# A spectral and state-space network on one core: rounding moved into PSUM, constant products taken out, instruction orders replaced

## The chip, the core and the metric

The kernel runs on one core of a Trainium2 chip. The core has a matrix engine, TensorE (PE in the profile, with its weight loads as PEld), which writes only to the accumulator memory PSUM; VectorE (DVE), ScalarE (ACT) and GpSimd (POOL), which work elementwise; and SyncE (SP), which here only issues transfers (DMAs) between the chip's main memory (HBM) and the on-chip memory SBUF. Each engine runs its own instructions in a fixed order and waits for the others through semaphores. The metric is the device time of one execution in microseconds, lower is better; the figure for the kernel before is the median of three timed runs.

## The reference

Four layers with a residual each, on `x` of 2048 rows and 512 columns. Layer A is a two-dimensional real FFT, a product with stored complex weights and the inverse FFT. Layer B is a diagonal state-space model (SSM): from parameters of 512 channels and 128 states it makes a convolution kernel `K` of length 2048 for each channel, and convolves with it by FFTs of length 4096. The normalized input goes into both. `K` is the same in both B layers.

```python
def _A_ref(x, w_r, w_i):
    X = jnp.fft.rfft2(x, axes=(-2, -1))
    return jnp.fft.irfft2(X * (w_r + 1j * w_i), s=(S, D), axes=(-2, -1))

def _B_ref(u, log_A_real, A_imag, C_real, C_imag, log_dt, D_skip):
    A = -jnp.exp(log_A_real) + 1j * A_imag
    C = (C_real + 1j * C_imag) * dt[:, None]
    P = jnp.exp((A * dt[:, None])[:, :, None] * pos[None, None, :])
    K = 2.0 * jnp.einsum("dn,dnl->dl", C, P).real
    Kf, Uf = jnp.fft.rfft(K, 2 * L), jnp.fft.rfft(u_t, 2 * L)
    y = jnp.fft.irfft(Uf * Kf[None, :, :], 2 * L)[:, :, :L]
    return y.transpose(0, 2, 1) + u * D_skip[None, None, :]

x = x + _A_ref(_layernorm(x), A_w_r, A_w_i)
x = x + _B_ref(_layernorm(x), ...)
x = x + _A_ref(_layernorm(x), A_w_r, A_w_i)
x = x + _B_ref(_layernorm(x), ...)
```

## The kernel before

All FFTs are products with small tables of sines and cosines on TensorE. Nearly every product is made in two halves (`halves`, L330, and `side_by_side`, L336): 64 columns of weights go to the left half of TensorE's array and 64 to the right half, and two such products run side by side. Products over 128 rows use two such halves of 128 by 64; some products of layer B and of the SSM's transform (those with the table `t`) use only 64 rows and run four at a time as 64 by 64. The profile names these shapes 128*64 and 64*64. A float32 product shows as two rows in the profile.

Layer A runs in three steps of 16 to 18 rounds: `spread` (layer norm and the first transform), `middle` (`forward`, `weigh`, `back`: the second transform, the product with the weights on DVE, the way back) and `end` (`fold`, `rows_back`). Layer B runs over four blocks of 128 channels: `rows` (64-row products), a copy by ACT and a transpose by DVE to the tile `z`, `pair` (products `p<-z,mb`), `weigh` (DVE products with `K`'s transform, then sums of 64x512 on POOL or DVE to `u`), and back through `units` (`p<-mb,u`) and `rows` (`p<-u,t`).

The SSM kernel is made beside the first layers A and B. `kernel_parts` turns the parameters into bfloat16 parts, written to HBM and read back as `th`. `kernel_time` then goes over 32 units of 16 channels, in groups of four, each unit in two halves, so 64 half units. Of each unit `grow` makes magnitudes: products `pk<-kb,th` of 512 columns, exponentials on ACT to `mag`. Of each half unit `bend` (L853) makes the phase, counted in turns, in one PSUM bank, `pk`: two pairs of products of 256 columns (`pk<-kb,th`). To bring it near zero DVE rounds the phase to the next integer (L864, `kw<-pk`: add and subtract 1.5 times 2 to the 23rd, `MAGIC`), and TensorE subtracts the integer from the same bank by a pair of products with minus the identity (`pk<-kw,ni`, 512 columns). Then ACT takes the absolute value and the sine (`sine`, `kf<-pk` and `pk<-pk`) and the cosine (`qp<-kf`), DVE multiplies with the magnitudes (`terms`, L886 and L888), and TensorE sums over the states (`total`, L899, `pv<-qp`). There are three `pk` banks and one `pv` bank. `kernel_freq` transforms `K` and stores it.

The order of the instructions is written out: `TURNS` holds for each engine a list of numbers, positions of the instructions as the program text makes them, and `take_turns` sets each engine's order by it. `ROOMS` holds, for every tile that the pools give out, which of the buffers of its name it takes. `WARM` holds, for some PSUM tiles, how many pairs of products of a constant (`self.warm`, ones) are made into the tile ahead of its real products (in `ps`); they are overwritten and nobody reads them. There are 231 such pairs, 924 rows in the profile. Transfers are issued by SP in its own order; the constants `kb` and `ni` are sent by POOL's queue, since they are converted to bfloat16 on the way.

Of the kernel before, what the change touches and what calls it, by code (L numbers as in the profile page):

```python
# [12 lines left out]
ALU = mybir.AluOpType  # L13
# [78 lines left out]
def constants():  # L92
# [111 lines left out]
    out["ni"] = -np.eye(128)  # L204
    out["kb"] = kb.reshape(96, 2560)
# [47 lines left out]
class Net:  # L253
# [553 lines left out]
    def kernel_constants(self):  # L807

        BF = mybir.dt.bfloat16
        self.kb = self.sb("kb", [2560], dt=BF, rows=96)  # L810
        self.ni = self.sb("ni", [128], dt=BF)
        self.nc.gpsimd.dma_start(self.kb, self.cst["kb"])
        self.nc.gpsimd.dma_start(self.ni, self.cst["ni"])

    def kernel_time(self, parts, kt, units, group):
# [6 lines left out]
        KQ, RM, RN, KP, RP = (KB[:, k:k + 512] for k in range(0, 2560, 512))  # L822
# [32 lines left out]
        def bend(i, j):  # L855
# [8 lines left out]
            nc.vector.tensor_scalar(whole, p, MAGIC, -MAGIC, op0=ALU.add, op1=ALU.add)  # L864
            self.halves(p, self.ni, whole, start=False, stop=True, skip_group_check=True)
            live[i, j] = p, mag

        def sine(i, j):
# [3 lines left out]
            ordered(p, p, ACT.Sin, scale=-TAU)  # L872
# [251 lines left out]
def net_kernel(ctx, tc, x, w, ends, kin, log_dt, d_skip, out, **cst):  # L1124
# [19 lines left out]
    with ExitStack() as outer:  # L1144
        with ExitStack() as early:
            early.enter_context(net.phase("pk", P, pk=(2048, PK), pv=(2048, PV)))
            with net.phase("p", P, p1=(2048, 8 - PK - PV), p2="p1", p3="p1"), \
                    net.phase("a", x=(32768, 1), ta=(8192, 1), ca=(6912, 1), u=(16384, 2), w=(2056, WA), wt=(2056, WT),
                              wv="w", junk="w"):
                A = net.layer_a(w, src=xv, dst=hd)  # L1150
                early.enter_context(net.phase("k0", side="right", kb=(5120, 1), ni=(256, 1), th=(1536, TH)))
                net.kernel_constants()
                with net.phase("v", val=(10240, 1), hp=(HP, 2)):
# [5 lines left out]
                    early.enter_context(net.phase("k", side="right", kw=(1024, 2), mag=(6144, MAG),  # L1159
# [10 lines left out]
            outer.enter_context(net.phase("b", t2=(8192, 1), u=(16384, 2), kk=(2048, 8), ta="t2", wt="w", wb="w", xw="w"))  # L1170
# [61 lines left out]
0-17 23-24 18-19 25-28 20-21 32-39 22 29-31 40-65 67-70 76-79 66 80-81 71-72 82-83 73-75 85-88 94-95 84 89-92  # L1232
103-106 93 96-97 112-113 107-108 98-101 109-110 102 114-115 111 116-119 121-124 120 125-126 130-131 127-128
132-133 129 134-161 172-179 163-168 180-181 169-171 182-193 162 194-211 218-219 234-235 212-217 220-221 236-241
222-225 242-249 256-259 226-231 260 264-266 250 267 251 261 232 268-272 252 262 273 253 263 233 274-279 298-307
280-281 254 312 282 286 255 313 287 314 288 315 289 283-285 308-311 316-321 290-291 322-331 338-339 292-295
340-342 346-349 343-345 296-297 350-351 332-335 366-371 358-365 336-337 374-387 414-417 372-373 402-413 418-423
464-465 424-427 388-393 448-451 466-467 452-455 476-483 512-513 456-461 514-515 394-397 516-517 398-401 462-463
428-431 518-519 432-433 520-523 434 436-437 435 438-439 352-357 548-551 554-557 524-525 468-475 552-553 440-441
484-487 558 492-494 504 495 559 505-507 488-491 442-447 496-497 526-533 498-499 508-511 500-503 534-543 560-561  # L1240
544-547 562-564 568 580 569 581 570 582 571 583 565-567 606-609 572-573 586-593 574-577 584 594 578 612 579 595
613 585 610 596-597 611 614-617 620-621 618-619 598-599 626-627 600-601 622-623 628 634-635 629-630 636-637
631-633 654-657 602-605 638-639 660-667 624-625 640-643 658 668-670 688 671 689 659 690-691 646-651 672-673
652-653 644-645 674-677 694-701 678 702-704 692 705 693 679 738-741 706-711 680-685 752-757 712 760 758 761 759
713 742-743 686 762-763 687 764-771 798-800 808-809 801-807 810-811 772-773 812 834-837 813-815 714-721 774-775
784-785 816-819 838-839 786-787 722-729 788-791 840-843 792-795 730-737 844-845 796-797 820-823 826-831 854-857
878 900-902 832-833 744-749 858-863 750-751 910 824-825 846-849 776-777 850-851 778-783 942 903 852-853 904-906
879-880 886-887 864-875 888 881-884 907-908 943-944 894-896 889-890 945 876-877 946-948 885 909 897 911-912
891-893 926-936 949 898 937-938 913-914 939 915-917 899 970-973 940-941 918-925 974-975 962-969 950-961 976-983
986-987 1032-1033 988-989 984-985 990-997 1006-1009 1034-1035 1010-1015 1054-1055 998-1003 1036-1039 1004-1005  # L1250
1056-1057 1076-1077 1040-1043 1016-1023 1044-1045 1066-1067 1024-1031 1078-1081 1068-1075 1046-1051 1082-1083
# [296 lines left out]
```

## Time and profile before

| | us |
|---|---|
| median of three timed runs | 716.46 |
| the three runs | 716.46, 710.45, 718.14 |
| span of the profiled execution, first to last instruction | 713.4 |

The profiled execution has no time of its own beside its span; the span lies inside the spread of the three runs, 3.1 us below their median.

The profile names an engine's instructions by line, operation, the tiles written and read and their shapes, with a count; "busy us, mean ns" are the time in which at least one of the group ran and the mean duration of one. Since products overlap, a group's busy time is less than count times mean. After it stand the engine's idle time just before these instructions and who ended it. In the tables of windows each engine's busy time stands with its number of instructions, then the share of TensorE's full clock that was granted (PEclk), the mean busy share of the DMA engines and the GB/s moved. A timeline row has a start, a duration, the engine, the line and the number of instructions merged into it.

### The profile page before, as it was taken

What the parts mean: (1) busy time and instruction counts of PE and PEld (TensorE: products, weight loads), DVE (VectorE), ACT (ScalarE), POOL (GpSimd) and SP (SyncE); (2) the same over time, 40 slices, a digit from 0 to 9 for tenths busy, and PEclk for the clock granted to TensorE, in tenths of its full rate; (3) what the DMA queues carried; (4) which work ended last, traced back from release to release, by engine and by line L of the source; (5) the groups of instructions that cost most, each with busy time, mean ns of one, the idle gap of its engine ahead of it and who ended that gap; (6) DMA issues with size and microseconds to landing.
All of it is one profiled execution on the core that took longest, in us unless ns stands there. A gap on an engine that the chain in (4) does not pass through costs nothing. (4 is left out here: it accounts for less than half of the span.)

```text
span 713.4 us, 23503 instructions
## 1 busy us (share of the span) xinstructions
PE 626.0 (88%) x9580; PEld 491.3 (69%) x9580; DVE 601.9 (84%) x1348; ACT 438.2 (61%) x946; POOL 357.3 (50%) x565
## 2 busy tenths in 40 slices
PE   4459989989996999889999997984989899999996
PEld 3237867878674867667858876774877766577876
DVE  4998497998999799969999676869588699799993
ACT  3558999997664796778868524333767427333322
POOL 1533528672852704543196356452056484286870
PEclk9779999999999999999999999997999999999999
DMA  8602611613558350455544689222123103335514
GB/s 282 229 0 89 210 48 47 122 62 43 167 133 245 107 138 32 65 128 94 163 62 136 195 198 246 80 106 75 61 77 89 46 2 104 125 103 149 156 34 111
DMA packets 137355, 81.32 MB, mean 114 GB/s; under 512 B 70976, under 2 KB 116928, under 8 KB 136352
## 3 DMA queue, kind: packets, MB, share of 16 engines
q1 hardware_dynamic: 136992, 79.30, 40.1%
q8 instruction: 76, 1.25, 0.7%
q0 software_dynamic: 256, 0.52, 0.4%
q14 instruction: 31, 0.25, 0.1%
HBM read 54.90 MB, written 25.43 MB: 113 GB/s over the span
## 5 line engine op out<-in xcount | busy, mean ns | idle before, releaser
L1003 POOL TENSOR_TENSOR u<-wb,wb 64x512 f32<-64x512 f32 x90 | 123.2, 1373 | 66.0 <-DVE wb L991 60.9
L336 PE MATMUL p<-z,mb 128*64 128x512 f32 (+2 forms) x480 | 108.0, 517 | 1.7 <-DVE wb L991 1.3
L899 PE MATMUL pv<-qp 128*64 128x128 f32 x1024 | 81.6, 279 | 5.0 <-ACT stage L907 4.2
L991 DVE TENSOR_TENSOR wb<-p,kk 128x512 f32<-128x512 f32 x128 | 81.5, 676 | 4.3 <-POOL u L1003 2.3
L336 PEld LDWEIGHTS p<-mb,u 128*64 128x64 f32 x2048 | 73.1, 138 | 13.1 <-issue 6.7
L336 PE MATMUL p<-mb,u 128*64 128x64 f32 x2048 | 74.3, 223 | 4.4 <-issue 2.0
L663 ACT COPY z<-p 128x512 f32<-128x512 f32 x96 | 52.4, 595 | 41.8 <-PE p L336 31.6
L669 DVE STREAM_TRANSPOSE z<-z 128x512 f32<-128x512 f32 x96 | 59.3, 675 | 19.8 <-ACT z L663 19.7
L899 PEld LDWEIGHTS pv<-qp 128*64 128x64 f32 x1024 | 64.4, 139 | 15.8 <-ACT stage L907 6.9
L1113 POOL TENSOR_SCALAR w<-w,norms 128x128 f32<-128x128 f32 x64 | 34.7, 554 | 67.7 <-DMA w<-h 29.8
L547 POOL TENSOR_TENSOR w<-w,w 64x257 f32<-64x257 f32 x48 | 34.7, 724 | 66.8 <-DVE w L542 45.3
L1015 ACT COPY u<-p 128x512 f32<-128x512 f32 x64 | 35.9, 590 | 48.7 <-PE p L336 45.3
L330 PE MATMUL p<-w,w 128*64 128x256 f32 x256 | 38.2, 438 | 27.8 <-DVE w L463 11.6
L330 PE MATMUL pk<-kb,th 96*64 96x256 bf16 (+1 forms) x384 | 56.5, 312 | 1.5 <-DVE qp L888 1.1
L542 DVE TENSOR_TENSOR w<-wt,p 128x514 f32<-128x514 f32 x64 | 42.7, 688 | 17.1 <-PE p L336 9.6
L864 DVE TENSOR_SCALAR kw<-pk 128x512 bf16<-128x512 f32 x64 | 42.9, 680 | 16.5 <-PE pk L330 16.1
L330 PE MATMUL p<-warm 128*64 128x128 f32 x612 | 49.2, 284 | 3.2 <-DVE half L1139 1.1
L336 PE MATMUL p<-t,w 64*64 64x128 f32 x1024 | 42.1, 280 | 10.2 <-DMA w<-kt 3.5
L336 PEld LDWEIGHTS p<-z,mb 128*64 128x64 f32 x480 | 39.7, 137 | 16.1 <-issue 7.9
L330 PEld LDWEIGHTS p<-w,w 128*64 128x64 f32 x256 | 24.7, 156 | 36.3 <-DVE w L463 12.7
L336 PE MATMUL p<-w,ca 128*64 128x257 f32 x256 | 45.0, 385 | 4.1 <-ACT w L526 1.5
L832 ACT ACTIVATE kf<-pk 128x512 f32<-128x512 f32 x64 | 38.8, 606 | 15.4 <-PE pk L330 13.8
(179 smaller groups left out, 1617.1 us busy)
## 6 DMA issues: line engine op xcount, KB each, us to landing
wt<-in_w SPq DMA_DIRECT2D x32, 257.0 KB, 2.7
kf<-kk SPq DMA_DIRECT2D x32, 256.0 KB, 3.3
kk<-kf SPq DMA_DIRECT2D x32, 256.0 KB, 2.7
u<-in_x SPq DMA_DIRECT2D x16, 256.0 KB, 6.8
hr<-in_x SPq DMA_DIRECT2D x16, 256.0 KB, 3.9
kt<-stage SPq DMA_DIRECT2D x32, 128.0 KB, 5.2
h<-hr SPq DMA_DIRECT2D x16, 256.0 KB, 3.0
w<-kt SPq DMA_DIRECT2D x32, 128.0 KB, 3.1
```

Of the source, the lines that this page charges most:

```text
L330: self.nc.tensor.matmul(out[64 * r:64 * r + 64], weights[:, 64 * r:64 * r + 64], data, **k)
L336: last = self.nc.tensor.matmul(out, weights, data, start=not more, stop=True, skip_group_check=True).ins
L542: nc.vector.tensor_mul(m[pl], W, px[:, None, :].to_broadcast([128, 2, 257]))
L547: e[0].tensor_sub(Y[0:64, v], m[0][hs, 0], m[1][hs, 1])
L663: nc.scalar.copy(tiles["z"][:, :, :, b, m:m + 2].rearrange("p u j m r -> p (u j) (m r)"), ps[b].rearrange("p u j m r -> p (u j) (m r)"))
L669: nc.vector.transpose(tiles["zt"][:, u:u + 8].rearrange("p u j d -> p (u j d)"), tiles["z"][:, u:u + 8].rearrange("p u j b m r -> p (u j b ...
L832: nc.scalar.activation(*a, **k)
L864: nc.vector.tensor_scalar(whole, p, MAGIC, -MAGIC, op0=ALU.add, op1=ALU.add)
L899: nc.tensor.matmul(p[64 * t:64 * t + 64, g], QP[:, c, 2, d:d + 2].rearrange("p s a -> p (s a)"), QP[:, c, 0:2, d:d + 2].rearrange("p k s b ...
L991: nc.vector.tensor_mul(split(m[c, pl], "du", [32, 16]), by_channel(p), split(k[c], "du", [32, 16]))
L1003: self.added = e[0].tensor_sub(y[0:64], v[0, 0], v[1, 1]), e[1].tensor_add(y[64:128], v[0, 1], v[1, 0])
L1015: nc.scalar.copy(V[:, :, j, :, d:d + 8].rearrange("p n q d -> p q n d"), p.rearrange("p (q n) d -> p q n d", q=2))
```

## The change

Four things change together.

The rounding. `bend` no longer has DVE round. TensorE makes the phase in the bank, adds `MAGIC` to every element of it and subtracts it again by products of a constant tile `big` (all `MAGIC`) with the first row of ones, then of minus ones, in `ni` (two pairs of 512 columns), so that the bank holds the rounded phase, and then adds the phase a second time with the sign turned (`LQ`, `LP`, new columns of `kb`: two pairs of 256 columns). The bank then holds the integer minus the phase, and the sine takes the scale plus 2 pi instead of minus 2 pi. `kw` is gone; `kb` grows from 2560 to 3584 columns, `ni` from 128 to 256, and POOL fills `big` once.

The constant products. `WARM` is empty, so `ps` makes none.

The pools. `phase` asks for every numbered room when it opens; some names in the calls stand in another order. This sets addresses.

The orders. All five lists of `TURNS`, and `ROOMS`, are new.

```diff
-    out["ni"] = -np.eye(128)
-    out["kb"] = kb.reshape(96, 2560)
+    first = np.zeros((128, 2, 128))
+    first[0, 0], first[0, 1] = 1, -1
+    out["ni"] = first.reshape(128, 256)
+    out["kb"] = np.concatenate([kb, -kb[:, :, :512], -kb[:, :, 1536:2048]], 2).reshape(96, 3584)
...
             for tag, v in tags.items():
                 self.tags[tag] = self.tags[v] if isinstance(v, str) else (pool, name, tag, *v)
+            for tag, v in tags.items():
+                if not isinstance(v, str):
+                    for k in range(v[1]):
+                        room = f"{tag}{k}" if v[1] > 1 else tag
+                        pool.tile([128, v[0] // 4], F32, tag=room, bufs=1, name=f"{name}_{room}")
...
-        self.kb = self.sb("kb", [2560], dt=BF, rows=96)
-        self.ni = self.sb("ni", [128], dt=BF)
+        self.kb = self.sb("kb", [3584], dt=BF, rows=96)
+        self.ni = self.sb("ni", [256], dt=BF)
+        self.big = self.sb("big", [512], dt=BF)
+        self.nc.gpsimd.memset(self.big, MAGIC)
...
-        KQ, RM, RN, KP, RP = (KB[:, k:k + 512] for k in range(0, 2560, 512))
+        KQ, RM, RN, KP, RP, LQ, LP = (KB[:, k:k + 512] for k in range(0, 3584, 512))
...
-            whole = self.sb("kw", [512], dt=BF)
             p = self.ps("pk", [2, 256])
-            self.halves(p[:, 0], th[:, h, 0], KQ[:, e], start=True, stop=False, skip_group_check=True)
-            self.halves(p[:, 1], th[:, h, 1], KP[:, e], start=False, stop=False, skip_group_check=True)
+            a, b = th[:, h, 0], th[:, h, 1]
+            self.halves(p[:, 0], a, KQ[:, e], start=True, stop=False)
+            self.halves(p[:, 1], b, KP[:, e], start=False, stop=False)
+            p0, p1 = p[:, 0], p[:, 1]
             p = p.rearrange("p k d -> p (k d)")
-            nc.vector.tensor_scalar(whole, p, MAGIC, -MAGIC, op0=ALU.add, op1=ALU.add)
-            self.halves(p, self.ni, whole, start=False, stop=True, skip_group_check=True)
+            self.halves(p, self.ni[:, 0:128], self.big, start=False, stop=False)
+            self.halves(p, self.ni[:, 128:256], self.big, start=False, stop=False)
+            self.halves(p0, a, LQ[:, e], start=False, stop=False)
+            self.halves(p1, b, LP[:, e], start=False, stop=True)
...
-            ordered(p, p, ACT.Sin, scale=-TAU)
+            ordered(p, p, ACT.Sin, scale=TAU)
...
-0-17 23-24 18-19 25-28 20-21 32-39 22 29-31 40-65 67-70 76-79 66 80-81 71-72 82-83 73-75 85-88 94-95 84 89-92
...
-WARM = {22: 7, 35: 3, 55: 1, 104: 3, 116: 2, 120: 5, 123: 6, 146: 2, 158: 1, 160: 2,
...
+WARM = {}
```

What the new orders do at three places follows. A row has the line in its own kernel (the helpers are L330 and L336 before, L337 and L343 after), the operation, the tile written and the tiles read with their numbers, the shape, a count, and the engines whose semaphores it waits for. Rows that repeat are left out.

The first half unit of the SSM kernel on PE, before (bank `pk_779`; `warm` is the constant, `ca`, `x` and `w` belong to layer A):

```order
L330 LDWEIGHTS th_679
L330 MATMUL pk_779<-kb_88,th_679 64x256 [waits Activation_49]
L330 MATMUL p_146_829<-warm_71 64x128 x4
L336 MATMUL p_146_829<-w_756,ca_745 64x257 [waits Activation_49]
L336 MATMUL p_148_838<-w_756,ca_745 64x257 x2
L330 LDWEIGHTS ni_89 [waits DMASW1_49]
L330 MATMUL pk_779<-kw_778,ni_89 64x512 [waits DVE_49]
```

and after (bank `pk_772`):

```order
L337 MATMUL pk_772<-kb_117,th_699 64x256 [waits Activation_49]
L480 MATMUL p_109_662<-w_653,edge_158 64x128 [waits DVE_49]
L337 MATMUL pk_735<-kb_117,th_725 64x512 [waits Activation_49]
L337 LDWEIGHTS ni_118 [waits DMASW0_49]
L337 MATMUL pk_772<-big_119,ni_118 64x512
L337 LDWEIGHTS th_699
L337 MATMUL pk_772<-kb_117,th_699 64x256
```

The wait for DVE between the phase and its rounding is gone, and the four pairs that follow wait for no engine. The same place on DVE, before:

```order
L801 TENSOR_TENSOR val_248<-val_248,hp_944 128x1920 [waits Activation_49]
L864 TENSOR_SCALAR kw_778<-pk_779 128x512 [waits PE_49]
L542 TENSOR_TENSOR w_836<-wt_763,p_146_829 128x514 [waits DMAHW0_49,PE_49]
L542 TENSOR_TENSOR w_841<-wt_763,p_148_838 128x514 [waits DVE_49,PE_49,Pool_49]
L864 TENSOR_SCALAR kw_797<-pk_798 128x512 [waits PE_49]
```

and after:

```order
L549 TENSOR_TENSOR w_839<-wt_757,p_147_836 128x514 [waits DMAHW1_49,PE_49,Pool_49]
L549 TENSOR_TENSOR w_834<-wt_757,p_145_831 128x514 [waits DVE_49]
L554 TENSOR_TENSOR w_841<-w_834,w_839 64x257 [waits DVE_49,Activation_49]
L898 SCALAR_TENSOR_TENSOR qp_808<-pk_795,mag_701 128x256 [waits Activation_49]
L898 SCALAR_TENSOR_TENSOR qp_785<-pk_772,mag_701 128x256
```

DVE's first work on a bank is now the product with the magnitudes.

The end of the second layer A (`ca,u` and `wv,ta`) and the start of the last layer B (`t,x`, the 64-row shape) on PE, before:

```order
L330 MATMUL p_1540_8438<-wv_8359,ta_8054 64x512 [waits DVE_49,Pool_49]
L336 MATMUL p_1584_8574<-t_8052,x_8056 64x64x2 [waits DMAHW4_49,Activation_49]
L330 MATMUL p_1585_8575<-warm_71 64x128 x4
L336 MATMUL p_1585_8575<-t_8052,x_8056 64x64x2
L336 MATMUL p_1584_8574<-t_8052,x_8056 64x64x2 [waits Activation_49]
```

and after:

```order
L343 MATMUL p_1521_8520<-t_8016,x_8020 64x64x2 [waits DMAHW4_49,Activation_49]
L343 MATMUL p_1522_8521<-t_8016,x_8020 64x64x2
L337 MATMUL p_1477_8394<-wv_8323,ta_8018 64x512 [waits DVE_49,Pool_49]
L343 MATMUL p_1521_8520<-t_8016,x_8020 64x64x2 [waits Activation_49]
L337 MATMUL p_1487_8426<-ca_6802,u_7368 64x256 [waits DVE_49,PE_49]
L337 MATMUL p_1491_8444<-wv_8346,ta_8018 64x512 [waits DVE_49,Pool_49]
L337 MATMUL p_1487_8426<-ca_6802,u_7368 64x256
```

Layer B's first products now stand between layer A's last ones, with a change of tile shape each time, and the two halves of the pair `p_1487` stand apart. Over the whole order PE changes between 128-row and 64-row products 92 times before and 154 times after, and 243 products before and 343 after go to the same half of the array, in the same shape, as the product ahead of them.

The first transfers on SP, before (`raw` are the SSM's parameters, `u` the rows of `x`, `ta` a table):

```order
L428 DMA u_83<-in_x 128x512 x5
L322 DMA ta_118<-in_ta 128x512
L739 DMA raw_247<-in_kin 128x2048
L428 DMA u_83<-in_x 128x512
L740 DMA raw_247<-in_log_dt 128x4 [waits DMAHW0_49]
```

and after:

```order
L435 DMA u_107<-in_x 128x512 x4
L746 DMA raw_264<-in_kin 128x2048
L747 DMA raw_264<-in_log_dt 128x4
L329 DMA ta_155<-in_ta 128x512
L435 DMA u_107<-in_x 128x512
```

The parameters now go ahead of the table and of the fifth row block.

More of the change, by code (lines that the diff above doesn't have):

```diff
@@ L1147, in net_kernel @@
             with net.phase("p", P, p1=(2048, 8 - PK - PV), p2="p1", p3="p1"), \
-                    net.phase("a", x=(32768, 1), ta=(8192, 1), ca=(6912, 1), u=(16384, 2), w=(2056, WA), wt=(2056, WT),
+                    net.phase("a", x=(32768, 1), u=(16384, 2), ta=(8192, 1), w=(2056, WA), ca=(6912, 1), wt=(2056, WT),
                               wv="w", junk="w"):
                 A = net.layer_a(w, src=xv, dst=hd)
-                early.enter_context(net.phase("k0", side="right", kb=(5120, 1), ni=(256, 1), th=(1536, TH)))
+                early.enter_context(net.phase("k0", side="right", kb=(7168, 1), ni=(512, 1), big=(1024, 1), th=(1536, TH)))
                 net.kernel_constants()
@@ L1158, in net_kernel @@
                     net.end_weights(ends)
-                    early.enter_context(net.phase("k", side="right", kw=(1024, 2), mag=(6144, MAG),
+                    early.enter_context(net.phase("k", side="right", mag=(6144, MAG),
                                                   qp=(6144, QP), kf=(2048, KF), stage=(8192, 1)))
@@ L1169, in net_kernel @@
             outer.enter_context(net.phase("f", t=(16384, 1), z=(16384, 2), w=(2056, WB)))
[L1170 removed]
+            outer.enter_context(net.phase("b", kk=(2048, 8), t2=(8192, 1), u=(16384, 2), ta="t2", wt="w", wb="w", xw="w"))
             pm = [int(c) for c in PM.split(",")]
@@ L1237 @@
[L1237 to L1241, printed above, removed]
```

461 lines of the change are left out of this document (225 added, 236 removed), and 9 rows, old and new, of the table WARM.

## The prediction

> **What bounds the kernel now.** I read the page's busy shares first, then the windows cut at the joints of the program, then the groups by shape, last the PE timeline.
>
> ```profile
> span 713.4 us, 23503 instructions
> PE 626.0 (88%) x9580; PEld 491.3 (69%) x9580; DVE 601.9 (84%) x1348; ACT 438.2 (61%) x946; POOL 357.3 (50%) x565
> PEclk9779999999999999999999999997999999999999
> ```
>
> Two engines are nearly full, TensorE (PE) and VectorE (DVE). The windows tell where. 0:70 is the start, 70:407 the stretch in which the SSM kernel is made (first `pk` product at 70.7 us), 407:492 the rest of the first layer B, 492:605 the second layer A, 605 on the last layer B.
>
> ```profile
> core 0: us, PE busy (x) PEld busy (x) DVE busy (x) ACT busy (x) POOL busy (x), PEclk, DMA share, GB/s
> 0.00:70.00 70.00, 40.73 (x318) 29.44 (x320) 57.30 (x151) 39.61 (x88) 25.17 (x59) 0.85 0.46 150
> 70.00:407.00 337.00, 312.21 (x4630) 246.33 (x4628) 299.87 (x663) 264.50 (x539) 172.26 (x292) 0.99 0.44 113
> 407.00:492.00 85.00, 69.04 (x1304) 56.00 (x1300) 64.16 (x151) 30.34 (x61) 45.36 (x47) 0.97 0.60 162
> 492.00:605.00 113.00, 104.89 (x1366) 81.95 (x1368) 90.94 (x233) 66.39 (x189) 52.96 (x122) 0.98 0.21 60
> 605.00:713.40 108.40, 99.16 (x1972) 77.55 (x1968) 89.61 (x154) 37.33 (x74) 61.52 (x45) 0.99 0.38 112
> ```
>
> The same windows, for the constant products (tile `warm`) alone:
>
> ```profile
> 70.00:407.00 337.00, 48.08 (x608) 36.49 (x608) 0.00 (x0) 0.99 0.44 113
> 492.00:605.00 113.00, 6.42 (x88) 4.95 (x88) 0.00 (x0) 0.98 0.21 60
> 605.00:713.40 108.40, 4.22 (x48) 2.93 (x48) 0.00 (x0) 0.99 0.38 112
> ```
>
> So in 70:407 DVE works 89% of the time, and PE 312 us, of which 48 are filling: its own work is 264 us, 78%. DVE sets the pace there, and PE waits and fills its waits. After 492 no SSM work is left, PE's own work is 98 of 113 and 95 of 108 us, and the change only reorders.
>
> **The change part by part.** The groups by shape give the prices:
>
> ```profile
> L864 DVE TENSOR_SCALAR kw<-pk 128x512 bf16<-128x512 f32 x64 | 42.9, 680 | 16.5 <-PE pk L330 16.1 <-PE p L336 0.2
> L832 ACT ACTIVATE kf<-pk 128x512 f32<-128x512 f32 x64 | 38.8, 606 | 15.4 <-PE pk L330 13.8 <-ACT z L663 0.3 <-ACT stage L907 0.2
> L330 PE MATMUL pk<-kb,th 96*64 96x256 bf16 x256 | 31.1, 274 | 0.6 <-DVE qp L888 0.5
> L330 PE MATMUL pk<-kw,ni 128*64 128x512 bf16 x128 | 29.3, 382 | 2.4 <-DVE kw L864 2.2
> L336 PE MATMUL p<-w,ca 128*64 128x257 f32 x256 | 45.0, 385 | 4.1 <-ACT w L526 1.5 <-POOL w L547 1.2 <-POOL w L519 0.6
> L832 ACT ACT_TABLE_LOAD x16 | 20.5, 1283 | 0.3
> ```
>
> 1. Rounding leaves DVE: 64 x 0.680 = 42.9 us, all in 70:407, with up to 16.1 us in which DVE waited for the product to round. DVE's work there falls to 299.9 - 42.9 = 257 us.
>
> 2. Rounding enters PE. Per half unit (64 of them) one pair of 512-column products against `ni` becomes two, and the two pairs of 256-column products run a second time. Back to back, a pair's price is the distance to the next start:
>
> ```profile
> 250.08 0.41 PE L330 MATMUL pk<-kw,ni 128*64 128x512 bf16 x2
> 250.29 1.07 PE L330 MATMUL p<-warm 128*64 128x128 f32 x16
> 251.17 1.08 PE L336 MATMUL p<-z,mb 128*64 128x32 f32 x6
> ...
> 258.32 0.28 PE L330 MATMUL pk<-kb,th 96*64 96x256 bf16 x2
> 258.43 0.39 PE L899 MATMUL pv<-qp 128*64 128x128 f32 x4
> ```
>
> A 512 pair takes 250.29 - 250.08 = 0.21 us, a 256 pair 0.11, so 0.21 + 2 x 0.11 = 0.43 us, and 64 x 0.43 = 27 us. That is the lower end; if every group stood alone with its whole latency, the groups above give 31.1 + 29.3 = 60.4 us. I take 27, because in the new order the added products stand as runs of two to four pairs on the same bank and wait for no engine.
>
> 3. The constant products go: 48.1 us of PE in 70:407, none of them needed by anybody. They filled waits, so nothing is credited for them except that PE is free when its inputs come early.
>
> 4. Tile shapes. In the two orders PE changes between products of 128 rows and of 64 rows 92 times before and 154 after; 48 of the 62 new changes lie ahead of the second layer A, 14 behind. One change is priced by eight constant products ahead of a 64-row product:
>
> ```profile
> 609.43 0.66 PE L330 MATMUL p<-warm 128*64 128x128 f32 x8
> 610.02 1.10 PE L336 MATMUL p<-t,x 64*64 64x128 f32 x22
> ```
>
> 16 such products take 251.17 - 250.29 = 0.88 us where no change follows, so eight take 0.44; here they take 0.59. A change costs 0.15 us: +7.2 us of PE ahead of the second layer A, +2.1 behind.
>
> 5. The order. Ahead of the SSM stretch the two table loads that the new order saves (24 before, 22 after) are 2 x 1.28 = 2.6 us of ScalarE (ACT), and the load of `raw` stands ahead of that of `ta` on SP's queue, so the chain that makes `parts` starts earlier; what it displaces is the first rows' normalization, which PE waits for there. Between 0 (PE and ACT hide it) and -3 us; I take -2. The larger `kb`, sent by POOL after the first edges instead of before them, is needed only by the first `pk` product at 70.7 us: nothing. The filling of `big` and the pools that take all rooms when they open put no instruction on PE, DVE or ACT: nothing, with POOL's idle half as the cover.
>
> Now the sum for 70:407. DVE 257 us, ACT 264.5, PE 312.2 - 48.1 + 27 + 7 = 298 us. PE becomes the fullest engine. How full an engine in the lead gets is read from two rows: DVE led 70:407 with 89%, PE, filling counted, showed 93%. PE takes its products in one fixed order as DVE takes its work, but it has now lost one partner in the loop, since a phase goes PE, ACT, DVE instead of PE, DVE, PE, ACT, DVE (the 13.8 us that ACT's first step waited for PE go too). I take 94%: 298 / 0.94 = 317 us, a gain of 20; with 89% it is 335 (gain 2), with 97% 307 (gain 30). Start -2, shape changes behind +2, the rest of the reordering nothing, since after 492 PE's own work is 193 of 221 us already. Sum: -20 us on a span of 713.4, so 693. The median of the timed runs, 716.5, stands 3.1 us over the span (the page gives no other time of the profiled run): 697.
>
> **The clock.** Some constant products kept TensorE's clock up.
>
> ```profile
> 312.40:315.90 3.50, 1.79 (x38) 1.25 (x38) 1.92 (x3) 2.06 (x6) 1.76 (x5) 0.99 0.96 217
> 315.90:319.30 3.40, 3.40 (x32) 2.71 (x32) 0.00 (x0) 2.43 (x6) 3.21 (x5) 0.51 0.40 110
> 292.00:295.40 3.40, 2.06 (x12) 0.75 (x12) 3.40 (x7) 2.43 (x6) 3.25 (x3) 1.00 0.58 91
> ...
> 561.60:565.00 3.40, 3.29 (x58) 2.86 (x53) 2.75 (x7) 1.29 (x4) 2.30 (x4) 1.00 0.00 0
> 73.50:76.90 3.40, 3.40 (x56) 3.24 (x55) 0.00 (x0) 3.40 (x7) 1.97 (x3) 1.00 0.09 28
> ```
>
> And of the last two of these windows, the constant products alone:
>
> ```profile
> 561.60:565.00 3.40, 1.92 (x28) 1.65 (x28) 0.00 (x0) 1.00 0.00 0
> 73.50:76.90 3.40, 3.15 (x44) 2.67 (x44) 0.00 (x0) 1.00 0.09 28
> ```
>
> After 3.5 us with 1.79 busy the clock is half for 3.4 us; after 3.4 with 2.06 busy it stays. PE's own work is 3.40 - 3.15 = 0.25 us in the window at 73.5 and 3.29 - 1.92 = 1.37 in the one at 561.6. These are the first and the last of seven windows that I found to lie below the border without their constant products; each then costs at most half of 3.4 us, so 0 to 12 us. I take 0, because the added 27 us of rounding lie in the same stretch, and keep 12 as a rival. The Trainium skill ("TensorE: Matmul & The Clock Gate", "Why this matters for your kernels") has another border: one whole idle window returns the clock to half. By that rule the constant products protected nothing here and the term is 0 without any argument. The trace of before does not bear it out: the window at 312.4 was half busy.
>
> **The rivals.**
>
> PE takes the whole gain. If PE, in the lead, gets no fuller than DVE did (89%), 298 us need 335, and with 60.4 instead of 27 us of rounding and the 94% of above (331 / 0.94 = 352) even more than before; in between lies no change: 714 to 718. For it: PE's products wait on four other engines. Against: its waits before were DVE's lateness. Chance 0.18.
>
> Slower: one half of the array idles. Products come in pairs, one for each 64-column half, that run side by side. In the new order 343 products go to the same half as the one ahead of them, 243 before; single products of a pair are issued as their inputs come. Each new one loses between one pass of 512 bf16 columns (0.21 us) and one 257-column f32 product (two rows each, so 45.0 us for 128 of them, 0.35 us), so 21 to 35 us. It decides from the point at which PE's 298 reaches 317 (317 / 0.94 = 337), 19 us, which all 100 at the lower price just pass; at the upper, 333 / 0.94 = 354, +17 over before: 734. For it: the count. Against: a split may stand in a time in which PE would wait anyway, and the order before has splits too. Chance 0.17.
>
> The clock falls in seven windows: 697 + 12 = 709. Chance 0.10.
>
> DVE's load was all that held it: 70:407 shrinks by the whole 42.9, as far as PE can follow (97%, 307 us), and the second layer A and last layer B, where the new order lets layer B's first products stand between layer A's last ones, give up a third of their 28 us of PE waits and filling: 697 - 10 - 9 = 678. Chance 0.12.
>
> **How the numbers follow.** The forecast's chance is 0.43, with 685 to 706 as its own range (97% and 92% in the leading stretch, 2 us either way at the start). A measurement here can tell about 1% from no change, so the bounds are 709.3 and 723.6. Faster: 0.43 + 0.12 + 0.10 = 0.65. Within: 0.18. Slower: 0.17. The range goes from 674, a little below the fast rival, to 728, half way into the slow one; what is left out is about 0.1 above and 0.05 below.
>
> **What would show it.** The SSM stretch runs from the first `pk` product to the last `pv` product, 341 us:
>
> ```profile
> 70.70 0.52 PE L330 MATMUL pk<-kb,th 96*64 96x512 bf16 x2
> ...
> 411.64 1.09 PE L899 MATMUL pv<-qp 128*64 128x128 f32 x16
> ```
>
> After: no DVE row `kw`, `pk<-kb,th` with 512 products of 256 columns, `pk<-big,ni` with 256, PE's added busy time between 27 and 60 us. Right: that stretch is 310 to 325 us long, with PE over 92% and DVE near 80%. Wrong: that stretch unchanged with PE's idle time as before (the wait was a chain's, not DVE's load), or PE full and the stretch as long as before (idle halves), or PEclk under 9 in slices between 8 and 38 (the clock), or a gain that lies behind the second layer A.

## The result, and the profile after

The changed kernel takes 710.46 us (median of 20 runs, 708.36 to 714.26) against 717.65 us for the kernel before (20 runs, 710.45 to 719.83). The ratio is 0.992, 95% interval 0.9902 to 0.9938: 0.8% faster, some 6 us by the ratio and 7.2 by the medians. The forecast was 697.0 us; the time lies in its range, and the gain is about a third of the one forecast.

The page of the changed kernel, its first lines and its row of TensorE's clock (40 slices of 17.8 us, tenths of full speed):

```profile
span 711.2 us, 22287 instructions
PE 636.6 (90%) x9040; PEld 464.6 (65%) x9040; DVE 576.2 (81%) x1284; ACT 434.8 (61%) x944; POOL 355.6 (50%) x566
PEclk9689999999999999999999999978999997999999
```

VectorE (DVE) lost 602 - 576 = 26 us of work, TensorE (PE) gained 11, although all constant products went. The windows, cut at the same joints as before: the first `pk` product, the last `pv` product, the first product of the second layer A, the end of its last, the end. Each row has the stretch, its length, and the busy time of the five engines, then the clock, the DMA share and the GB/s:

```profile
0.00:65.50 65.50, 36.17 (x258) 21.57 (x260) 55.97 (x148) 36.24 (x87) 25.44 (x58) 0.87 0.50 165
65.50:390.20 324.70, 314.45 (x4454) 239.47 (x4450) 271.10 (x602) 263.85 (x535) 168.31 (x289) 1.00 0.45 114
390.20:480.10 89.90, 72.24 (x1137) 47.78 (x1136) 65.51 (x148) 31.43 (x63) 48.93 (x52) 0.95 0.62 164
480.10:589.70 109.60, 103.45 (x1284) 81.68 (x1287) 93.06 (x228) 65.01 (x186) 52.75 (x123) 0.98 0.17 48
589.70:711.20 121.50, 110.31 (x1920) 74.15 (x1920) 90.56 (x162) 38.26 (x76) 60.15 (x45) 0.96 0.37 112
```

The kernel before, cut at these joints:

```profile
0.00:70.70 70.70, 41.43 (x325) 29.95 (x326) 57.86 (x152) 40.31 (x90) 25.17 (x59) 0.86 0.46 150
70.70:412.70 342.00, 317.21 (x4735) 250.40 (x4732) 301.05 (x669) 267.64 (x543) 173.99 (x296) 0.99 0.45 117
412.70:492.00 79.30, 63.34 (x1195) 51.42 (x1193) 62.41 (x143) 26.50 (x53) 43.62 (x43) 0.97 0.56 148
492.00:605.70 113.70, 105.59 (x1372) 82.26 (x1374) 91.54 (x237) 67.00 (x190) 52.96 (x122) 0.98 0.21 60
605.70:713.40 107.70, 98.46 (x1970) 77.24 (x1964) 89.02 (x150) 36.72 (x73) 61.52 (x45) 0.99 0.38 112
```

Stage by stage, after less before: -5.2, -17.3, +10.6, -4.1, +13.8. The SSM stretch is 17.3 us shorter, but 9 us of TensorE's work now stand behind its end, in a stretch that is 10.6 us longer; the two together give 6.7. At the end of the second layer A the changed kernel is 605.7 - 589.7 = 16.0 us ahead. In the last layer B, where neither the rounding nor the SSM has any work, it loses 13.8 of them. There TensorE's busy time rose by 11.9 us, although the layer computes the same and its constant products are gone. That is where to look first. One caution: the two profiled executions stand 713.4 - 711.2 = 2.2 us apart and the medians 7.2, so some 5 us of such stage differences can be chance between executions; the 13.8 us are more than that.

### The profile page after: what moved, and what is told of

Its sections match the earlier page's. It is cut to its first block, busy times and chain, and to the rows that moved or that the text cites. A ratio compares the mean times of both kernels' runs of the same rounds, so it can differ in the third digit from the quotient of the medians.

```text
span 711.2 us, 22287 instructions
## 1 busy us (share of the span) xinstructions
PE 636.6 (90%) x9040; PEld 464.6 (65%) x9040; DVE 576.2 (81%) x1284; ACT 434.8 (61%) x944; POOL 355.6 (50%) x566
## 5 line engine op out<-in xcount | busy, mean ns | idle before, releaser
L343 PE MATMUL p<-z,mb 128*64 128x512 f32 (+2 forms) x480 | 139.0, 525 | 1.8 <-DVE z L676 1.7
L911 PE MATMUL pv<-qp 128*64 128x128 f32 x1024 | 99.7, 276 | 1.7 <-ACT stage L919 1.2
L337 PE MATMUL pk<-kb,th 96*64 96x256 bf16 (+1 forms) x640 | 90.7, 296 | 4.3 <-DMA th<-parts 2.1
L911 PEld LDWEIGHTS pv<-qp 128*64 128x64 f32 x1024 | 73.1, 136 | 17.3 <-issue 6.6
L343 PEld LDWEIGHTS p<-mb,u 128*64 128x64 f32 x2048 | 69.5, 140 | 15.6 <-issue 12.2
L343 PE MATMUL p<-mb,u 128*64 128x64 f32 x2048 | 72.8, 226 | 6.5 <-issue 2.5
L337 PEld LDWEIGHTS <-th 96*64 96x64 bf16 x640 | 49.2, 109 | 24.1 <-issue 10.0
L337 PE MATMUL p<-w,w 128*64 128x256 f32 x256 | 38.2, 432 | 28.5 <-ACT w L465 17.4
L1027 ACT COPY u<-p 128x512 f32<-128x512 f32 x64 | 36.8, 590 | 41.4 <-PE p L343 41.3
L549 DVE TENSOR_TENSOR w<-wt,p 128x514 f32<-128x514 f32 x64 | 42.3, 687 | 22.6 <-PE p L343 17.3
L343 PEld LDWEIGHTS p<-z,mb 128*64 128x64 f32 x480 | 40.9, 138 | 29.8 <-issue 18.7
L337 PE MATMUL p<-ca,u 128*64 128x128 f32 (+2 forms) x512 | 56.2, 301 | 0.4 <-ACT u L570 0.3
L337 PE MATMUL p<-ca,w 128*64 128x128 f32 x512 | 52.6, 276 | 2.8 <-DVE w L556 1.2
L343 PE MATMUL p<-w,ca 128*64 128x257 f32 x256 | 52.4, 385 | 2.0 <-ACT w L533 1.2
L343 PEld LDWEIGHTS p<-t,w 64*64 64x64 f32 x1024 | 33.0, 132 | 28.1 <-issue 15.2
L337 PEld LDWEIGHTS p<-ca,u 128*64 128x64 f32 x512 | 43.2, 136 | 11.9 <-issue 6.4
L343 PE MATMUL p<-t,w 64*64 64x128 f32 x1024 | 46.4, 280 | 5.1 <-ACT z L670 2.6
```

The costliest lines, as they stand in the source:

```text
L337: self.nc.tensor.matmul(out[64 * r:64 * r + 64], weights[:, 64 * r:64 * r + 64], data, **k)
L343: last = self.nc.tensor.matmul(out, weights, data, start=not more, stop=True, skip_group_check=True).ins
L549: nc.vector.tensor_mul(m[pl], W, px[:, None, :].to_broadcast([128, 2, 257]))
L911: nc.tensor.matmul(p[64 * t:64 * t + 64, g], QP[:, c, 2, d:d + 2].rearrange("p s a -> p (s a)"), QP[:, c, 0:2, d:d + 2].rearrange("p k s b ...
L1027: nc.scalar.copy(V[:, :, j, :, d:d + 8].rearrange("p n q d -> p q n d"), p.rearrange("p (q n) d -> p q n d", q=2))
```

## The experiments

The changed kernel wasn't timed again beside these runs. The kernel before was, and its medians, 717.29 to 718.82 us against the 717.65 above, say how far times of different runs can be compared: to some 2 us.

**What the last layer B loses, by its order alone.** Theory A was that products for the two halves of the array stand apart in the new order, so that one half idles; theory B that the clock falls, since the layer has no constant products; theory C the tile shapes. The order's instructions can be told from one another by the step that makes them, so an order can be put together from both kernels at a point that both pass without overlap. The point taken is the fifth fold of the second layer A. The first run is the changed kernel up to there, and has the order and the rooms of the kernel before from there on. In the rooms of the last `z,mb` banks one sees where it turns:

```diff
-    "pc.p2": "1012120121200210201202100201021210210210122121021012012010201201",
+    "pc.p2": "1012120121200210201202100201021202102102102102102102102102102102",
```

> The changed kernel up to the fifth fold of the second layer A, and from there on the order and the rooms of the kernel before, without its constant products. Theory A (idle array halves): in the changed order the products that fill the two halves of the array stand apart in the last layer B, which makes its in-order stream 11 us longer, and 20 more tile-shape changes at 0.10 to 0.15 us add 2 to 3; with the old order both go, so 711 - 11 to 14, 697 to 700 us. Theory B (clock): the three half-clock windows at 594.8 to 605 us cost up to 5 us and come of the missing constant products; they are missing here too, so 707 to 711 us. Theory C (tile shapes alone): 3 us, 707 to 709 us.

Measured: 701.3 us, ratio 0.9756 (0.9694 to 0.9818), just above theory A's range and well below those of B and C. The converse is the kernel before with the change's order from that point on, where the 26 pairs of constant products go too:

```diff
-    "pc.p2": "2102102102102102102102102102102102102102102102102102102102102102",
+    "pc.p2": "2102102102102102102102102102102110210210122121021012012010201201",
```

> The converse: the kernel before up to the fifth fold of the second layer A, with its rounding and its constant products, and from there on the order and rooms of the changed kernel and no constant products. Theory A (idle halves): 717 + 11 to 14, with the clock up to 5 more: 728 to 736 us. Theory B (clock alone): 717 + 4 to 5, 721 to 722 us. If what is lost in the last layer B hangs on what comes ahead of it, and not on its own order: 717 us.

Measured: 730.35 us, ratio 1.0137 (1.0068 to 1.0207). The last layer B of the first run, in the old order:

```profile
589.40:700.80 111.40, 100.41 (x1922) 78.64 (x1920) 90.60 (x163) 38.55 (x77) 61.34 (x45) 0.93 0.38 109
```

and of the second, in the new one:

```profile
607.00:728.40 121.40, 110.40 (x1922) 74.23 (x1920) 91.49 (x162) 38.23 (x76) 60.03 (x45) 0.96 0.37 112
```

The old order gives 111.4 us, the new one 121.4, whatever comes ahead, and the shorter one has the lower clock (0.93 against 0.96). So the loss belongs to the layer's own order. This doesn't yet tell idle halves from tile shapes, since the old order has fewer of both.

**The pairs alone.** In the changed order 20 of the 32 `z,mb` tiles of the last layer B have their products apart. The third run puts them together on TensorE and moves nothing else; 40 of the 44 tile-shape changes stay. At one place (the difference between the two orders, - changed kernel, + this run):

```
-L343 MATMUL p_1564_8766<-z_8600,mb_3188 64x512
 L337 MATMUL p_1559_8722<-u_8517,mb_3188 64x32 x2
-L343 MATMUL p_1564_8766<-z_8600,mb_3188 64x512
-L343 MATMUL p_1567_8773<-z_8600,mb_3188 64x512
+L343 MATMUL p_1564_8766<-z_8600,mb_3188 64x512 x2
 L343 MATMUL p_1574_8840<-t_8016,x_8020 64x64x2
...
-L343 MATMUL p_1567_8773<-z_8600,mb_3188 64x512
+L343 MATMUL p_1567_8773<-z_8600,mb_3188 64x512 x2
```

> The changed kernel; in the last layer B alone each z,mb tile's two or three products stand together on TensorE, at the place of the last of them; nothing else moves, and 40 of the 44 tile-shape changes stay. Theory A: the in-order stream of the last layer B falls by 11 us, nearly all of it on the path, since TensorE is busy there without a gap: 699 to 703 us. Theory B (clock) and theory C (tile shapes): 710 us, at most 1 us less.

Measured: 698.51 us, ratio 0.9711 (0.9646 to 0.9776), 12 us below the changed kernel, as theory A said; theories B and C are out as the main cause. The price of one lone product stands in TensorE's timeline (start, duration, shape, rows; two rows are one float32 product). In the changed kernel:

```profile
616.27 1.04 PE L343 MATMUL p<-z,mb 128*64 128x512 f32 x2
617.25 1.10 PE L343 MATMUL p<-t,x 64*64 64x128 f32 x32
```

and in the run with the pairs joined:

```profile
608.50 1.08 PE L343 MATMUL p<-z,mb 128*64 128x512 f32 x4
609.50 0.68 PE L343 MATMUL p<-t,x 64*64 64x128 f32 x4
```

One product alone ahead of a change of shape holds TensorE for 617.25 - 616.27 = 0.98 us; a pair, twice the work, for 1.00. Nothing fills the other half meanwhile: the next product has another shape and starts only behind it. A pair split in this way costs 1.96 us instead of 1.00, 0.48 more for each of its two products. Not every split product is alone, since some stand beside one of another tile; 12 us are the price of some 25 such products. The Trainium skill ("TensorEngine Tiling (Array Packing)", "Key Properties") says that a change of the tiling mode drains the engine and that different tiles work in parallel. The rows fit both: a pair takes no longer than one product, and the next shape starts only when the lone one is done. With 40 shape changes this run's last layer B is no longer than that of the first run with 24, at a clock of 0.95 against 0.93:

```profile
591.50:702.00 110.50, 101.12 (x1920) 73.35 (x1920) 89.48 (x162) 38.06 (x76) 61.49 (x45) 0.95 0.42 124
```

**All pairs.** Ahead of the last layer B the changed order splits 40 more `z,mb` tiles, 50 pairs in the middle steps and 64 in the folds of layer A. The fourth run joins them all, again on TensorE alone. One place in the middle steps, where the two products of `p_156` had the bfloat16 products of a half unit between them:

```
-L343 MATMUL p_156_893<-w_821,ca_739 64x257
 L337 LDWEIGHTS th_699
 L337 MATMUL pk_852<-kb_117,th_699 64x256
...
-L343 MATMUL p_156_893<-w_821,ca_739 64x257
+L343 MATMUL p_156_893<-w_821,ca_739 64x257 x2
```

> The changed kernel with every pair of products for the two halves of the array that its order splits (folds, middle steps, z,mb products of all blocks) joined again, on TensorE alone; 145 of 155 tile-shape changes stay. Theory A: idle halves cost in the layers ahead of the last too; an in-order count of the array's halves gives 60 us of idle for the changed order, 10 for the order before and 8 here. The last layer B gives 8 to 11 us; ahead of it TensorE was over nine tenths busy, so that some of the rest shows: 685 to 697 us. If ahead of the last layer B waits set the pace and not the halves: as the run with only the last layer's pairs joined, 699 to 703 us.

Measured: 688.21 us, ratio 0.9568 (0.9509 to 0.9627): 4% below the kernel before, 3% below the changed one. The `z,mb` products of 512 columns, each time the same 288 rows (count, busy time, mean ns of one), in the kernel before:

```profile
L336 PE MATMUL p<-z,mb 128*64 128x512 f32 x288 | 101.0, 597 | 1.7 <-DVE wb L991 1.3 <-DVE z L669 0.3
```

in the changed kernel:

```profile
L343 PE MATMUL p<-z,mb 128*64 128x512 f32 x288 | 114.7, 608 | 1.8 <-DVE z L676 1.7
```

and in this run:

```profile
L343 PE MATMUL p<-z,mb 128*64 128x512 f32 x288 | 101.3, 604 | 1.2 <-DVE z L676 0.7 <-ACT kk L966 0.2
```

The means hardly differ; what changed is how many ran beside another.

**The rounding alone.** Ahead of the last layer the question was what brings the gain. The fifth run keeps the old order and all constant products and changes the rounding in `bend`, with its tables and the pools, whose part wasn't tried alone; the eight new products stand where the two `kw,ni` products stood:

```diff
-            nc.vector.tensor_scalar(whole, p, MAGIC, -MAGIC, op0=ALU.add, op1=ALU.add)
-            self.halves(p, self.ni, whole, start=False, stop=True, skip_group_check=True)
+            self.halves(p, self.ni[:, 0:128], self.big, start=False, stop=False)
+            self.halves(p, self.ni[:, 128:256], self.big, start=False, stop=False)
+            self.halves(p0, a, LQ[:, e], start=False, stop=False)
+            self.halves(p1, b, LP[:, e], start=False, stop=True)
```

> The kernel before, with its order, its rooms and all its constant products; only the rounding goes to TensorE, the eight new products standing where the two kw,ni products stood. By the forecast's terms TensorE takes 27 us more between the first pk and the last pv product and VectorE 43 us less. Theory A (the gain ahead of the second layer A is the rounding's; the order gave only the waits it needed and lost idle halves): 700 to 712 us. Theory B (without the new order the added products only stand in front of others): 717 to 735 us.

Measured: 741.81 us, ratio 1.0359 (1.0307 to 1.0411), more than even theory B expected: in the old order the rounding on TensorE is a loss of 24 us.

**The constant products alone.** The kernel before with its old order:

```diff
-WARM = {22: 7, 35: 3, 55: 1, 104: 3, 116: 2, 120: 5, 123: 6, 146: 2, 158: 1, 160: 2,
...
+WARM = {}
```

> The kernel before with its 231 pairs of constant products left out, nothing else. If they only fill waits and the clock holds without them: 712 to 717 us. If windows fall below the border (the earlier count gave up to seven, 1.7 us each): 717 to 729 us, with PEclk under 9 in slices between 4 and 24.

Measured: 709.61 us, ratio 0.9899 (0.987 to 0.9928), 1% faster, and better than either expectation. The granted clock is lower (0.948 to 0.957 in its eight executions, 0.955 to 0.975 in the eleven of the kernel before beside it), and the kernel is faster for all that. Not in every stage: its last layer B takes 109.9 us, where that of the kernel before takes 107.7.

```profile
598.70:708.60 109.90, 98.70 (x1920) 78.25 (x1920) 90.70 (x162) 38.58 (x77) 61.43 (x45) 0.95 0.38 111
```

On balance the constant products cost more than they gave; that they stood in the way of real products is the likely reading, and no run shows it apart.

**Rounding without constant products.** The whole change but for its order, so the last two edits together:

```diff
-WARM = {22: 7, 35: 3, 55: 1, 104: 3, 116: 2, 120: 5, 123: 6, 146: 2, 158: 1, 160: 2,
...
+WARM = {}
...
-            nc.vector.tensor_scalar(whole, p, MAGIC, -MAGIC, op0=ALU.add, op1=ALU.add)
...
+            self.halves(p, self.ni[:, 0:128], self.big, start=False, stop=False)
```

> The order and rooms of the kernel before, rounding by TensorE, no constant products: the whole change without its new order. Against the run with the constant products kept: if their place is taken by the rounding products, as the forecast put it, the same or up to 6 us less; if the clock needs them, up to 10 us more. Against the changed kernel (710 us): if the new order's idle halves cost more than the order brings, this is below 710; if the order brings more, above.

Measured: 734.3 us, ratio 1.025 (1.0195 to 1.0305), 24 us above the changed kernel: with the rounding on TensorE the new order, idle halves included, brings that much. The stretch from the first `pk` product to the first product of the second layer A follows for five kernels. The kernel before:

```profile
70.70:492.00 421.30, 380.55 (x5924) 301.82 (x5921) 363.46 (x812) 294.14 (x596) 217.62 (x339) 0.99 0.47 123
```

The run without constant products:

```profile
71.00:488.90 417.90, 356.76 (x5188) 264.23 (x5189) 361.51 (x812) 293.07 (x595) 216.75 (x339) 0.97 0.48 124
```

The run that has the rounding as well:

```profile
72.30:509.40 437.10, 379.29 (x5574) 291.66 (x5575) 331.82 (x748) 294.57 (x595) 214.97 (x339) 0.95 0.46 118
```

The change:

```profile
65.50:480.10 414.60, 386.69 (x5586) 287.25 (x5582) 336.61 (x750) 295.28 (x598) 217.23 (x341) 0.99 0.49 125
```

The change with all pairs joined:

```profile
64.60:467.30 402.70, 372.62 (x5584) 273.84 (x5580) 335.85 (x749) 294.50 (x598) 217.79 (x341) 0.99 0.50 129
```

Read the first two figures behind the bounds in each row, the length and TensorE's busy time. The rounding (second to third) adds 22.5 us of TensorE's work and takes 29.7 from VectorE; the stretch grows by 19.2, and TensorE idles as long as before (61.1 and 57.8 us). In the old order its waits were not cured by giving VectorE time. VectorE itself idles 56.4 us in the second row (417.9 - 361.5) and 105.3 in the third. Where that time went stands in its groups, without the rounding on TensorE (count, busy time, mean ns, then the idle time just before them and who ended it):

```profile
L864 DVE TENSOR_SCALAR kw<-pk 128x512 bf16<-128x512 f32 x64 | 42.8, 679 | 14.6 <-PE pk L330 14.3 <-PE p L336 0.2
L886 DVE SCALAR_TENSOR_TENSOR qp<-qp,mag 128x256 f32<-128x256 f32 x64 | 28.1, 448 | 0.4 <-ACT qp L832 0.4
L886 DVE SCALAR_TENSOR_TENSOR qp<-pk,mag 128x256 f32<-128x256 f32 x64 | 26.4, 412 | 3.1 <-ACT pk L832 2.9
L542 DVE TENSOR_TENSOR w<-wt,p 128x514 f32<-128x514 f32 x64 | 42.6, 688 | 15.0 <-PE p L336 9.2 <-POOL mag L848 1.4 <-POOL wt L530 0.8
```

and with it:

```profile
L898 DVE SCALAR_TENSOR_TENSOR qp<-qp,mag 128x256 f32<-128x256 f32 x64 | 33.3, 529 | 3.0 <-ACT qp L841 2.8
L898 DVE SCALAR_TENSOR_TENSOR qp<-pk,mag 128x256 f32<-128x256 f32 x64 | 26.7, 418 | 23.5 <-ACT pk L841 22.8 <-issue 0.3
L549 DVE TENSOR_TENSOR w<-wt,p 128x514 f32<-128x514 f32 x64 | 42.7, 689 | 34.7 <-PE p L343 25.4 <-POOL w L525 2.3 <-PE p L337 2.0
```

VectorE now waits for the others. It no longer waits for a phase to round (14.6 us), but for the sine of the same half unit, where 3.1 us of idle time became 23.5, and for layer A's products, `w<-wt,p`, where 15.0 became 34.7, most of it for TensorE. In the old order, which was made for the rounding on VectorE, the half units come no faster.

Back to the windows. The new order (third to fourth) halves the idle time, 57.8 to 27.9 us, but adds 7.4 us of busy time; the joined pairs (fifth) take 14.1 off that and keep the idle time at 30.1.

**The clock.** At the start of the last layer B the changed kernel runs at half clock for 10 us. The eighth run puts constant products into TensorE's waits there:

```diff
-WARM = {}
+WARM = {1532: 16}
```

The 16 pairs stand as 6, 2, 1, 5 and 2, ahead of the products that wait there.

> The changed kernel with 16 pairs of constant products put into the four waits of TensorE at the start of the last layer B (590.9 to 598.8 us), in the bank of the first z,mb tile; nothing else moves. If the three half-clock windows at 594.8 to 605 us cost what the order of VectorE's work shows between 594 and 608 us (14 us ahead falls to 10): 705 to 708 us. If products at half clock there only stand in front of waits that end when they end anyway: 709 to 711 us. A split-pair cause alone expects 710 us.

Measured: 708.39 us, ratio 0.989 (0.9841 to 0.994), which doesn't stand apart from the change's 0.992. Three windows of the changed kernel:

```profile
594.70:598.20 3.50, 1.95 (x20) 1.01 (x16) 0.79 (x2) 1.44 (x3) 0.00 (x0) 0.51 0.96 370
598.20:601.60 3.40, 2.83 (x11) 0.88 (x12) 3.40 (x6) 0.00 (x0) 0.00 (x0) 0.50 0.01 5
601.60:605.00 3.40, 3.40 (x21) 1.23 (x20) 0.67 (x2) 0.00 (x0) 0.00 (x0) 0.50 0.00 0
```

and of this run, with its whole last layer B:

```profile
592.90:596.30 3.40, 3.08 (x49) 2.13 (x47) 1.37 (x3) 1.19 (x3) 0.00 (x0) 1.00 0.95 348
596.30:599.80 3.50, 3.50 (x31) 1.31 (x32) 3.49 (x6) 0.00 (x0) 0.00 (x0) 1.00 0.03 11
587.70:706.00 118.30, 110.84 (x1984) 76.66 (x1984) 90.65 (x162) 38.23 (x76) 60.15 (x45) 0.99 0.38 116
```

The clock stays up, and the layer takes 118.3 us instead of 121.5. So the clock's part is about 3 us between these two profiles, and too small for the timed runs to show.

**Both together.** All pairs joined, without and with these constant products, on one chip; the edit of the second is that of the clock's run on top of the joined pairs:

```diff
-WARM = {}
+WARM = {1532: 16}
```

> The changed kernel with all split pairs joined, once more beside the one with the constant products, on the same chip: 688 us, ratio to the kernel before 0.952 to 0.962.

> The changed kernel with all split pairs joined, and the 16 pairs of constant products of the clock run at the start of its last layer B, where its PEclk falls to 8 and the windows at 578 to 588 us are at half clock. If the clock's cost there adds to the halves': 2 to 3 us below the joined kernel without them, 685 to 686 us. If, with the pairs together, the products behind the waits have room to catch up: no difference, 688 us.

Measured: 690.37 us, ratio 0.9611 (0.9578 to 0.9643), without; 688.56 us, 0.9576 (0.9546 to 0.9606), with. The intervals overlap, so whether the constant products help there stays open. Either beats both kernels by 3 to 4%.

## Why the prediction was right or wrong

The prediction gave -20 us, all of it from the rounding, with the order worth nothing behind the SSM stretch. The runs give, as one path of single steps (medians): constant products out -8 (709.6), rounding +25 (734.3), new order -24 (710.5). The sum is -7; the parts are not what the prediction took them for. Two of its steps failed: TensorE's own work, which made the rounding look free (1), and the idle halves of the new order, left out of the sum (4 and 5). That the time still came out faster, and inside the range, is luck: in this path the gain comes from the order and the missing constant products, against the rounding. With the pairs of the last layer B joined the time is 698.5 us, close to the forecast, and that would have been luck too.

1. "its own work is 264 us, 78%. DVE sets the pace there": the first failed step, and with it "Rounding leaves DVE" as a gain. The 264 us are TensorE's 312 less the 48 of the constant products. But products run side by side, so busy times of groups don't subtract: in the same trace and window the rows of the real products alone cover 287 us. Without the constant products the SSM stretch reads:

```profile
71.00:408.70 337.70, 296.29 (x4124) 217.52 (x4124) 300.13 (x669) 266.47 (x542) 172.93 (x296) 0.97 0.46 118
```

TensorE is busy for 88% of it and VectorE for 89%. With the rounding the stretch is 19.5 us longer, TensorE is 23.1 us busier and VectorE 29.7 less busy:

```profile
72.30:429.50 357.20, 319.35 (x4508) 245.54 (x4512) 270.39 (x605) 267.93 (x542) 171.21 (x296) 0.96 0.43 112
```

TensorE's idle time hardly took the added products in: 41.4 us without them, 37.9 with them. What the runs show in place of a gain is a stretch that grows by nearly all of TensorE's added work. The sum's own rule shows the size of the error: 319 us at 94% are 340 us, no gain on 337, and at 89% 359, about what was measured. So the rival "PE takes the whole gain" had the right mechanism for the old order, and even it was too mild there (742 us with the constant products kept). In the new order TensorE is filled to 97%, and what the rounding is worth there no run shows.

2. "Rounding enters PE", 27 us: about right in size, 22.5 measured as busy time, a little under what was called the lower end. The groups went from 31.1 + 29.3 us to those that follow, 49 us more, within the 27 to 60 named as a sign:

```profile
L337 PE MATMUL pk<-kb,th 96*64 96x256 bf16 x512 | 63.1, 274 | 2.1 <-DVE qp L900 1.8 <-ACT mag L841 0.2
...
L337 PE MATMUL pk<-big,ni 128*64 128x512 bf16 x256 | 46.2, 380 | 0.0
```

3. "nothing is credited" for the constant products: too low by 8 us in the medians. The rows of the kernel before and of the run without them show 421.3 - 417.9 = 3.4 us of it in the stretch to the second layer A, and in that layer, where before it took 113.7 us, 3.9 more (the row that follows); the last layer B, shown above, gave 2.2 back:

```profile
488.90:598.70 109.80, 100.06 (x1280) 77.85 (x1280) 89.85 (x225) 64.83 (x185) 52.95 (x122) 0.97 0.22 61
```

4. "the rest of the reordering nothing": the second failed step, wrong both ways. Ahead of the second layer A the order repaid the rounding; in the last layer B it cost 10 to 14 us.

5. The idle halves stood among the rivals, with 21 to 35 us and a chance of 0.17, as a case against the gain. They were a term of the sum: joining the pairs gave 12 us in the last layer B and 8 to 10 ahead of it, about the rival's lower end, while the gain beside them was real. The count behind it was also the wrong one. Without the constant products, those that go to the same half as the one ahead of them are 37 in the last layer B in the old order and 38 in the new one, so that count saw nothing where half of the cost lay. What costs, by the rows of the third run, is above all a lone product ahead of a change of shape. Step 4 of the sum priced 14 more shape changes there (20, if the constant products of before are left out) at 0.15 us, 2.1 in all, and left out the half that stays empty ahead of them.

6. TensorE's work of 298 us between 70 and 407, with 69 to the second layer A, 367, at 94%: 8.9 of the 69 are constant products, so the sum's figure is 358. As written the kernel has 386.7 us in 414.6, 93%; with all pairs joined 372.6 in 402.7, 93%. The step that made TensorE the fullest engine holds, and nearly so does its 94%. The work was 28 us too small: 14 of them are the split pairs; how the other 14 divide between the reading of step 1 and what else the sum left out stays open.

7. The signs. "that stretch is 310 to 325 us long, with PE over 92%": 324.7 and 97%, but 9 us of its work had moved out of it, and part of the 97% is one half working. "DVE near 80%": 83%. The start, forecast -2, gave -5.2. "PEclk under 9": slice 33 of the page (counted from 0), the start of the last layer B, is new; the dip in slices 26 and 27, around the start of the second layer A, was there before in one of them. The rival with seven fallen windows in the SSM stretch didn't come: the clock there is 1.00.

8. The Trainium skill's rule ("TensorE: Matmul & The Clock Gate", "Why this matters for your kernels") that one idle window returns the clock to half is not contradicted as a warning, but the changed kernel's clock fell behind the window at 591.3, which was not idle:

```profile
591.30:594.70 3.40, 1.38 (x20) 0.80 (x20) 2.45 (x15) 3.34 (x7) 0.00 (x0) 1.00 0.88 358
```

The window behind it is the first of those shown above, at 0.51.

Not settled: what the new order would give with the rounding left on VectorE. That wasn't tried, because it needs an order of its own. So the runs show that the rounding was a loss in the old order, not that it is one in the new.

## What to carry to other kernels

When an order is searched or written by hand, count the array's halves: two products that fill it stay next to each other, above all ahead of a change of tile shape, where a lone one costs as much as the pair (0.98 against 1.00 us). Before work is moved off a full engine, try the move alone: here it cost 25 us in the order that was made for the old place. Don't subtract busy times of groups that run side by side: 312 us less 48 of filling left 287, not 264. And where a change has several parts, price each stage's order by itself; a gain ahead can be given back in a stage that the change seems not to touch.

## What the hardware showed that was not expected

The constant products that kept the clock up cost more than they gave. Without them the granted clock fell from 0.967 to 0.954 (medians of the timed executions), and the time by 1% all the same (717.29 to 709.61 us). And a product alone on one half of the array shows the same duration in its rows as one with a neighbour (means of 597 to 608 ns); the loss stands only in the distance to the next start, and in a group's busy time (101.0 to 114.7 us for the same 288 rows). VectorE's multiplication `qp<-qp,mag`, of one shape and count, took 448 ns on the mean with the rounding on VectorE and 529 with it on TensorE; why wasn't tried.
